# The second layer of two early batches as seven quarter products, on one Trainium2 core

## The chip, the core and the metric

The kernel runs on one core of a Trainium2 chip. Its time is the device time of one execution in microseconds (us); a median of several executions is given, and one execution was recorded by the hardware profiler. The engines of the core are TensorE (PE in the rows, with its weight loads as PEld), VectorE (DVE), ScalarE (ACT), GpSimd (POOL) and SyncE (SP), which here only starts transfers. Each engine works through its own list of instructions in order, and waits where an input or a buffer is not ready. PE writes into eight accumulation banks of 128 rows by 512 float32; ACT and DVE read them and write to the on-chip memory.

## What is computed

For 8 batches of 8 heads with 512 tokens, 32 states and 64 features, tokens read from states and states read from tokens, both by a softmax. The 544 rows of a batch (512 token rows, then 32 state rows) then go through a layer with a maximum of two products, and a last product.

```
scores = scale * x @ state.T          ; scores -= max over states
a = exp(scores) / sum                 ; xread = a @ state
scores2 = scale * state @ x.T         ; scores2 -= max over tokens
a2 = exp(scores2) / sum               ; sread = a2 @ x
X = concat([xread, sread]) as (8 * 544, 512)
out = maximum(X @ w1, X @ w2) @ w_out
```

## The kernel before

**The algebra.** `maximum(X w1, X w2)` is written as `relu(X (w1 - w2)) + X w2`. So the kernel keeps `wd` = w1 - w2, `wwo` = w2 w_out and `wo` = w_out, and the result is `relu(X wd) wo + X wwo`. As xread = a @ state, it multiplies the states into the weights first: `sw` of a batch holds state times `wd` (1,024 columns, the parts 0 and 1 of `sw`) and state times `wwo` (512 columns, the part `w`). Layer one of a batch (`l1_mm`, eight pieces) multiplies `sw` by the transposed attention weights `at`; a relu copies each piece into `r`. Layer two multiplies `r` by `wo` and adds `at` times the part `w` of `sw`.

**Two ways through layer two.** Batches 2 to 7 go through it by a scheme with seven quarter products in place of eight (`product`, `opened`, `keep`, `put`): `r` and `wo` are cut into quarters, sums and differences of quarters are made (`r_sum` into `st`, `w_sum` into `wt`, `difference` into `dif`), three intermediate sums are copied out of the banks (`keep`, into `part`), and four quarters of the output are put together (`put`). Each product is eight matmuls of 256 columns. Batches 0 and 1 go through layer two directly (`l2_mm`): for each of four groups of 128 rows, eight matmuls with `wo` and two with `sw`, all of 512 columns, and one copy out (`l2_out`).

**The order of the work.** The work ahead of the loop over batches 2 to 7 is the list `ORDER`: each token is a call, with the engine behind `>` and the bank numbers behind `@`. `l1.1.5@6` is layer one of batch 1, piece 5, in bank 6; `re.1.5>V` its relu on VectorE; `sw.0.w` the product for the part `w` of batch 0 and `swe.0.w.1>A` the copy of one half of it on ScalarE; `sc`, `exp`, `red`, `mul` are scores, exponential, sums and normalisation; `xtd`, `atd`, `Sd` are transposing transfers, `ldx` loads of `x`, `ce` and `cb` casts of `x`. The list's order is the program order: every engine gets its instructions in it, and an instruction waits for what stands before it in the list and writes what it reads, or reads what it overwrites. `RELEASE` gives the order in which the loop takes up the banks.

**The state rows of batches 0 and 1.** Their numerators and sums are computed early (`srw`) and copied into `srx` (`swre`). They are picked out of it by eight small copies on GpSimd (`srp`, function `sr_pick`) into `srd`, and divided in the loop, with batches 2 and 3 (`sr_ev`). `srx` has no memory of its own: it is a view of the third `sw` buffer, which batch 2 uses as its `sw`.

```
srd = wz.bitcast(F32).rearrange("p (b z) -> p b z", b=2)
srx = sw_s[2].rearrange("p g w -> p (g w)")[:, 0:2080].bitcast(F32).rearrange("p (b g k z) -> p b g k z", b=2, g=2, k=4)
```

`sr_ev` writes the reciprocal of each sum into `rr_all`, which is a part of `sums`. A buffer of batch `b` is number `b % 3` for `sw`, `at` and `xe`, and `b % 2` for `r`, `e`, `a`, `xt` and `xb`.

**The guard and the general block.** The main path leaves out the subtraction of the maximum. So the kernel looks at every sum that it divided by, and at the reciprocals of the state rows:

```
sv = sums[:, 0:B * 34]
nc.vector.tensor_scalar(cl, sv, scalar1=1e-20, scalar2=1e20, op0=ALU.max, op1=ALU.min)
nc.vector.tensor_tensor(ne, cl, sv, op=ALU.not_equal)
nc.vector.tensor_reduce(bad, ne, axis=AXX, op=ALU.max)
```

A matmul adds `bad` over the 128 rows, the integer goes into `flag`, every engine loads it into a register, and behind the last batch stands `with tc.If(fv >= 1, ...)`. The block in it (`general`) does all eight batches again, one after the other, with the maxima subtracted, and the state rows too: each batch is loaded anew through GpSimd's queue into one buffer (`slot["x0"]`), goes through casts, transposes, scores, both softmaxes, `sw`, layer one and the direct layer two, and is stored through GpSimd's queue; the last state rows follow with `m1` and `m2`. In GpSimd's list the two stores of a batch stand ahead of the two loads of the next. In the execution shown below the block was not entered.

**The end.** `m1` and `m2` take the state rows of all batches through both layers in two groups of 128 rows. The last half of the second group is copied by DVE and ACT, 128 columns each.

Of the kernel before, what the change touches and what calls it, by code (L numbers as in the profile page):

```python
# [36 lines left out]
sw.0.0@2,4 re.0.4>V sw.1.0@0,5 swe.0.0.1>A sw.0.w@1,3 swe.1.0.1>V sw.1.w@7,6 ce.2.0>P swe.1.0.0>A l2.1.3.3@4  # L37
swe.1.w.0>V cb.2.1>P l2.1.2.3@5 swe.0.0.0>A l2.1.2.2@5 swe.1.w.1>V swe.0.w.1>A l1.1.2@2 ce.2.3>P xtd.2 mS.1>A
swe.0.w.0>V l2.1.3.2@4 ce.2.1>P l1.0.3@3 l1.0.1@1 re.1.2>A ce.2.2>P l1.1.0@6 re.0.3>A re.0.1>V l2.0.2.2@2 l1.0.6@7
re.1.0>V mS.0>A l1.1.3@1 l1.0.2@6 re.0.6>A Sd l2.0.3.o@3 ldx.4.1 re.0.2>A l2.1.3.o@4 ldx.3.0 l2.0.3.3@3 re.1.3>A  # L40
l1.0.0@6 ldx.4.0 l1.1.1@1 re.0.0>V l2.1.0.o@7 ldx.3.1 l2.1.0.2@7 re.1.1>V l2.0.0.1@6 l2.1.2.0@5 l2.1.0.0@7 l2.1.2.o@5
l2.0.0.o@6 sc.2.0@1 l2.0.3.1@3 exp.2.0>A l2.1.1.3@0 l2.0.2.o@2 red.2.0>V l2.1.3.1@4 l2.1.3.0@4 srp.0>P srp.1>P wt.0>P wt.2>P wt.1>P
mul.2.0>P l2.1.1.1@0 le.1.3>A sc.2.1@1 l2.1.1.2@0 ce.3.0>P exp.2.1>A l2.1.0.1@7 ce.3.1>P l2.0.2.3@2 red.2.1>V
l2.1.2.1@5 cb.3.0>P l2.0.3.0@3 le.1.2>V l2.0.0.3@6 mul.2.1>P l2.1.1.0@0 l2.0.0.2@6 l2.1.1.o@0 ce.3.3>P atd.2
l2.1.0.3@7 ce.3.2>P le.1.1>A l2.0.3.2@3 le.1.0>V l2.0.0.0@6 cb.3.1>P le.0.3>A sr.2@0 le.0.0>V sw.2.0@3,7 xtd.3
ldx.5.0 ldx.5.1
sw.2.w@5,1 sre.2>V swe.2.0.0>A sw.2.1@6,4 l2.0.2.0@2 swe.2.w.1>A swe.2.w.0>V l2.0.1.3@0 swe.2.1.1>A l2.0.2.1@2
swe.2.0.1>V l2.0.1.o@0 le.0.2>A l2.0.1.2@0 swe.2.1.0>A l2.0.1.0@0 srt.2@2 l2.0.1.1@0 srte.2>A le.0.1>V store.0
# [6 lines left out]
RELEASE = [3, 1, 5, 4, 7, 6, 2, 0]  # L55
# [3 lines left out]
def kernel(  # L59
# [9 lines left out]
    nc = tc.nc  # L69
# [494 lines left out]
    for b in range(2):  # L564
        for c in range(NC):
            left[f"l2{b}{c}"] = 5
# [276 lines left out]
```

## Time and profile before

| What | Time |
|---|---|
| median of 3 executions | 147.36 us (147.19 to 147.72) |
| the profiled execution, device time | 147.19 us |
| its span, first to last instruction | 145.4 us |
| PE busy in the span | 136.4 us of 145.4 (94%) |
| DVE, ACT, POOL busy | 98.3, 82.1, 67.9 us |
| last instruction of PE ends, then last of ACT | 140.3 us, 140.9 us |
| `flag` written by DVE | 120.3 us |

The rows of the trace give a start and a duration in us, the engine, the line (`L427` is line 427 of the kernel), the operation, what is written from what is read, and the tiles' sizes. Rows by line give a count, the busy time in us, and the mean of one instruction in ns. The chain of work that ended last is followed back from the last instruction. The 1.8 us between the device time and the span lie around the instructions.

### The profile page before, as it was taken

The numbers are of one execution on the slowest core, as the hardware profiler recorded it, in microseconds if no ns is written. First come the engines' busy times: TensorE is split into PE (matmuls) and PEld (weight loads), VectorE is DVE, ScalarE is ACT, GpSimd is POOL, SyncE is SP. The second block draws the span as 40 slices with busy tenths as digits, with TensorE's granted clock in tenths as the row PEclk, the third lists the DMA queues.
The fourth block names the chain that finished last, engine by engine and source line by source line (L and its number), as shares of the span: only waits on it lengthen the run. The fifth ranks groups of instructions, "written<-read, shape, count | busy, mean of one in ns | idle before, by whom it ended". The sixth has DMA issues, their size and how long they took to land.

```text
span 145.4 us, 3491 instructions
## 1 busy us (share of the span) xinstructions
PE 136.4 (94%) x1376; PEld 89.0 (61%) x1388; DVE 98.3 (68%) x181; ACT 82.1 (56%) x157; POOL 67.9 (47%) x95
## 2 busy tenths in 40 slices
PE   6888999999999999999999999999999999999950
PEld 2566735444454446785778478757867784885840
DVE  3488969783324648997899789489948896941300
ACT  4457789898122675845781768268556817831110
POOL 4147320198979990498079509923930630000000
PEclk9999999999999999999999999999999999999995
DMA  3999999939991599999976991487316034202451
GB/s 126 331 364 394 384 387 385 327 58 174 243 359 59 97 251 393 369 136 275 384 123 138 347 285 33 72 288 149 67 42 252 7 72 185 113 0 72 155 181 38
DMA packets 36468, 29.50 MB, mean 203 GB/s; under 512 B 22624, under 2 KB 32352, under 8 KB 35552
## 3 DMA queue, kind: packets, MB, share of 16 engines
q1 hardware_dynamic: 36176, 29.10, 68.9%
q8 instruction: 12, 0.20, 0.6%
q10 hardware_dynamic: 272, 0.13, 0.3%
q14 instruction: 8, 0.07, 0.2%
HBM read 15.20 MB, written 8.91 MB: 166 GB/s over the span
## 4 chain that ended last, share of the span: by engine, by line
PE 83%; DMA 11%; ACT 1%; issue 1%; DVE 1%; SPq 0%; DVEq 0%
PE bank L427 26%; PE bank L376 19%; PE bank L390 9%; DMA big<-in_moe_w_out_dram 8%; PE bank L433 7%; PE bank L353 4%; DMA big<-in_x_dram 3%; PE bank L578 3%; PE bank L474 2%; PE bank L484 2%; PE bank L385 2%; PE bank L265 2%; PE bank L305 1%; PE bank L482 1%; ACT wo L103 1%
## 5 line engine op out<-in xcount | busy, mean ns | idle before, releaser
L371 DVE TENSOR_SCALAR r<-bank 128x512 bf16<-128x512 f32 x32 | 21.8, 691 | 13.0 <-PE bank L376 12.6
L281 POOL TENSOR_TENSOR a<-e,er 128x512 bf16<-128x512 bf16 x14 | 16.6, 1195 | 29.5 <-ACT e L273 22.5
L376 PE MATMUL bank<-at,sw 128*128 128x512 bf16 x122 | 29.4, 379 | 0.5 <-DVE sw L105 0.2
L103 ACT COPY big<-bank 128x512 f32<-128x512 f32 (+1 forms) x29 | 16.9, 587 | 17.5 <-PE bank L427 6.6
L103 ACT CAST sw<-bank 128x512 bf16<-128x512 f32 x35 | 19.5, 606 | 4.0 <-PE bank L353 4.0
L427 PEld LDWEIGHTS <-big 128*128 128x128 bf16 x192 | 17.9, 98 | 5.1 <-DVE er L278 2.1
L369 ACT ACTIVATE r<-bank 128x512 bf16<-128x512 f32 x32 | 18.5, 597 | 4.5 <-PE bank L376 4.2
L376 PEld LDWEIGHTS <-sw 128*128 128x128 bf16 x128 | 12.3, 98 | 14.1 <-ACT sw L103 0.5
L107 POOL CAST xe<-big 128x512 bf16<-128x512 f32 x27 | 17.7, 688 | 6.2 <-DMA big<-in_x_dram 6.2
L427 PE MATMUL bank<-big,big 128*128 128x256 bf16 x144 | 17.1, 273 | 0.0
L107 POOL CAST xb<-big 128x1024 bf16<-128x1024 f32 x12 | 12.2, 1040 | 7.2 <-DMA big<-in_x_dram 7.2
L390 PE MATMUL bank<-wo,r 128*128 128x512 bf16 x61 | 15.2, 379 | 0.3 <-issue 0.2
L427 PEld LDWEIGHTS <-r 128*128 128x128 bf16 x144 | 13.7, 98 | 2.6
L403 DVE TENSOR_TENSOR big<-bank,big 128x512 f32<-128x512 f32 (+1 forms) x19 | 12.3, 654 | 2.9 <-PE bank L433 2.9
L277 DVE TENSOR_REDUCE sums<-e 128x16 f32<-128x512 bf16 x16 | 10.6, 664 | 5.1 <-ACT e L273 5.0
L103 ACT COPY sread_t<-bank 128x128 bf16<-128x128 bf16 x8 | 3.3, 473 | 16.9 <-PE bank L337 13.7
L273 ACT ACTIVATE e<-bank 128x512 bf16<-128x512 f32 x16 | 9.0, 601 | 5.8 <-PE bank L265 5.7
L427 PE MATMUL bank<-wo,r 128*128 128x256 bf16 x96 | 12.3, 273 | 0.0
L433 PE MATMUL bank<-sw,at 128*128 128x256 bf16 x72 | 10.8, 273 | 0.0
L390 PEld LDWEIGHTS <-r 128*128 128x128 bf16 x64 | 5.9, 98 | 7.0 <-issue 0.5
L433 PEld LDWEIGHTS <-at 128*128 128x128 bf16 x96 | 9.4, 98 | 1.1
L403 DVE TENSOR_TENSOR big<-r 128x1024 bf16<-128x1024 bf16 x12 | 9.2, 767 | 0.6
(86 smaller groups left out, 195.9 us busy)
## 6 DMA issues: line engine op xcount, KB each, us to landing
big<-in_x_dram SPq DMA_DIRECT2D x16, 512.0 KB, 5.5
out_dram<-big SPq DMA_DIRECT2D x7, 1024.0 KB, 5.4
big<-in_moe_w_dram SPq DMA_DIRECT2D x8, 512.0 KB, 11.7
big<-in_moe_w_out_dram SPq DMA_DIRECT2D x4, 512.0 KB, 11.7
out_dram<-big SPq DMA_DIRECT2D x4, 256.0 KB, 3.5
sf<-in_state_dram SPq DMA_DIRECT2D x1, 384.0 KB, 10.4
out_dram<-w2m SPq DMA_DIRECT2D x1, 256.0 KB, 2.5
out_dram<-w2m SPq DMA_DIRECT2D x2, 128.0 KB, 3.1
```

Of the source, the lines that this page charges most:

```text
L103: nc.scalar.copy(o, i)
L107: nc.gpsimd.tensor_copy(o, i)
L273: nc.scalar.activation(out=e_view(e_s[b % 2], hh).rearrange("p (g c) i n -> p g c (i n)", g=2), in_=p.rearrange("p (c g m) -> p g c m", c= ...
L277: nc.vector.tensor_reduce(es_all[:, b, hh], e_view(e_s[b % 2], hh), axis=AXX, op=ALU.add)
L281: (nc.gpsimd if eng == "P" else nc.vector).tensor_mul(e_view(a_s[b % 2], hh), e_view(e_s[b % 2], hh), er_s[b % 2][:, hh].unsqueeze(3).to_b ...
L369: nc.scalar.activation(out=o, in_=p, func=ACTF.Relu)
L371: nc.vector.tensor_scalar(o, p, scalar1=0.0, scalar2=None, op0=ALU.max)
L376: nc.tensor.matmul(p, sw_s[b % 3][:, g, f * 128:(f + 1) * 128], at_s[b % 3][:, g].rearrange("p c t -> p (c t)"), start=(g == 0), stop=(g = ...
L390: nc.tensor.matmul(p[:, lo:hi], r_s[b % 2][:, f, c * 128:(c + 1) * 128], wo[:, f, lo:hi], start=(start and j == 0), stop=(stop and j == le ...
L403: (nc.gpsimd if eng == "P" else nc.vector).tensor_tensor(o, i0, i1, op=op)
L427: nc.tensor.matmul(pv[c], lhs[:, f, 128 * c:128 * c + 128], rhs[:, f, :], start=first and f == 0 and (c == 0 or pv.split), stop=False, ski ...
L433: nc.tensor.matmul(pv[c], at_s[b % 3][:, g, 2 * i + c, :], rhs[:, g, :], start=False, stop=False, skip_group_check=True)
```

## The change

Batches 0 and 1 now go through layer two by seven quarter products as well. New tokens stand for the steps (`p1` to `p7` products, `p2o`, `o7`, `o3`, `o4` the terms with `sw`, `k0` to `k2` the copies into `part`, `rs` and `wt` the sums, `dif` the differences, `v00` to `v10` the outputs), and the second half of `ORDER` is written anew, with other banks and other engines for many copies; `RELEASE` is changed with it. The casts `ce.2` move from POOL to ACT, `wt.2` and `wt.3` from POOL to DVE, and `store.0` stands ahead of `xtd.3`. The state rows are ordered by batch and then by state within `sread_t` and in `m_store`, ACT alone makes the last copy, and the general block's last stores are cut in halves. The pieces of the diff, the list cut to the lines that the text speaks of:

```diff
-swe.0.w.0>V l2.1.3.2@4 ce.2.1>P l1.0.3@3 l1.0.1@1 re.1.2>A ce.2.2>P l1.1.0@6 re.0.3>A re.0.1>V l2.0.2.2@2 l1.0.6@7
-l2.0.0.o@6 sc.2.0@1 l2.0.3.1@3 exp.2.0>A l2.1.1.3@0 l2.0.2.o@2 red.2.0>V l2.1.3.1@4 l2.1.3.0@4 srp.0>P srp.1>P wt.0>P wt.2>P wt.1>P
...
+p1.0@1 k0.0>A p1.1@4 rs.0.2>V wt.2>V v00.0 p6.0 rs.0.3>V k0.1>A k1.0>A p5.0@7 wt.3>V v00.1 rs.1.0>V k2.0>A
+sc.2.0@6 exp.2.0>A sc.2.1@0 exp.2.1>A sw.2.0@5,3 red.2.0>V mul.2.0>P red.2.1>V swe.2.0.0>A swe.2.0.1>A ce.2.0>A ce.2.1>A ce.2.2>A ce.2.3>A
+p7.0 o7.0 v11.0 rs.1.1>V mul.2.1>P p3.0 o3.0 rs.1.2>V atd.2 sw.2.w@6,2 swe.2.w.0>A v01.0 swe.2.w.1>A
+p4.0 o4.0 rs.1.3>V ce.3.0>P ce.3.1>P cb.3.0>P ce.3.2>P ce.3.3>P cb.3.1>P v10.0>A store.0 xtd.3 dif.1>P
+sr.2@0 p6.1 k1.1>A sw.2.1@5,3 sre.2>V swe.2.1.0>A swe.2.1.1>V p5.1@7 k2.1>A srp.0>P srp.1>P
...
-RELEASE = [3, 1, 5, 4, 7, 6, 2, 0]
+RELEASE = [1, 6, 2, 5, 3, 0, 4, 7]
...
-        o = sread_t.rearrange("p k (t n q) -> p k t n q", t=2, q=4)
-        copy(eng, o[:, :, b // 4, :, b % 4], p[:, 0:128].rearrange("p (k n) -> p k n", k=4))
+        o = sread_t.rearrange("p k (t q n) -> p k t q n", t=2, q=4)
+        copy(eng, o[:, :, b // 4, b % 4, :], p[:, 0:128].rearrange("p (k n) -> p k n", k=4))
...
-        (eng or nc.sync).dma_start(out=out.rearrange("(t q l) m -> t l q m", t=2, l=L)[t, S:L, :, lo:hi],
+        (eng or nc.sync).dma_start(out=out.rearrange("(t q l) m -> t q l m", t=2, l=L)[t, :, S:L, lo:hi],
...
+    def fresh(kind, b, lhs, rhs, at):
+        pairs[kind, b] = Pair(at)
+        product(pairs[kind, b], lhs, rhs, True)
...
-    w_sum(3, "P")
...
-    m2(1, "VA", "r", 256, 512)
+    m2(1, "A", "r", 256, 512)
...
-            m_store(t, nc.gpsimd)
+            for k in range(2):
+                m_store(t, nc.gpsimd, 256 * k, 256 * k + 256)
```

POOL's list behind the first casts of batch 2, before. The eight copies `wz0<-sw2` are `srp.0` and `srp.1` (`srd` is a view of `wz`, `srx` one of `sw2`); `big3<-wo0` are the weight sums `wt`, `a0<-e0,er0` is `mul.2`, `xe0` and `xb1` from `big9` are the casts of batch 3, and `big6<-sw2` is `dif` of batch 2:

```order
L107 COPY wz0_73<-sw2_104 32x130 x8
L403 TENSOR_TENSOR big3_112<-wo0_77 128x1024 x2
L403 TENSOR_TENSOR big3_112<-wo0_77,big3_112 128x1024
L281 TENSOR_TENSOR a0_93<-e0_91,er0_95 128x8x64
L107 CAST xe0_84<-big9_118 128x2x4x64 x2
L107 CAST xb1_90<-big9_118 128x4x4x64
L281 TENSOR_TENSOR a0_93<-e0_91,er0_95 128x8x64
L107 CAST xe0_84<-big9_118 128x2x4x64 x2
```

The same stretch of POOL's list now, where a line number is one lower than before:

```order
L402 TENSOR_TENSOR big3_112<-wo0_77 128x1024
L106 CAST xb0_89<-big8_117 128x4x4x64
L402 TENSOR_TENSOR big3_112<-wo0_77,big3_112 128x1024
L402 TENSOR_TENSOR big6_115<-sw0_102 128x512
L280 TENSOR_TENSOR a0_93<-e0_91,er0_95 128x8x64 x2
L106 CAST xe0_84<-big9_118 128x2x4x64 x2
L106 CAST xb1_90<-big9_118 128x4x4x64
L106 CAST xe0_84<-big9_118 128x2x4x64 x2
L106 CAST xb1_90<-big9_118 128x4x4x64
L402 TENSOR_TENSOR big6_115<-sw1_103 128x512
L106 COPY wz0_73<-sw2_104 32x130 x8
L402 TENSOR_TENSOR big6_115<-sw2_104 128x512
```

The eight copies moved from ahead of `mul.2` and the casts of batch 3 to behind them, two weight sums left POOL, and `dif` of batches 0 and 1 (`big6<-sw0`, `big6<-sw1`) came in.

ACT's list around batch 2's scores, before. `e0<-bank` is `exp.2`, `sw2<-bank` are the copies `swe.2` of batch 2's products into the third `sw` buffer, and `big2<-bank`, `big0<-bank` are output copies of batches 1 and 0:

```order
L273 ACTIVATE e0_91<-bank1_64 128x8x64
L103 COPY big2_111<-bank0_63 128x512
L103 COPY big0_109<-bank3_66 128x512
L103 CAST sw2_104<-bank3_66 128x512
L103 CAST sw2_104<-bank1_64 128x512
L103 CAST sw2_104<-bank4_67 128x512
L103 COPY big0_109<-bank2_65 128x512
L103 CAST sw2_104<-bank6_69 128x512
```

ACT's list there now; `big6<-bank` are the copies `k` into `part`, and `xe2` the casts `ce.2`:

```order
L102 COPY big6_115<-bank7_70 128x512
L272 ACTIVATE e0_91<-bank6_69 128x8x64
L272 ACTIVATE e0_91<-bank0_63 128x8x64
L102 CAST sw2_104<-bank5_68 128x512
L102 CAST sw2_104<-bank3_66 128x512
L102 CAST xe2_86<-big8_117 128x2x4x64 x4
L102 CAST sw2_104<-bank6_69 128x512
L102 CAST sw2_104<-bank2_65 128x512
L102 COPY big0_109<-bank1_64 128x2x256
L102 COPY big6_115<-bank4_67 128x512
L102 CAST sw2_104<-bank5_68 128x512
```

Two of the copies into `sw2` now stand directly behind the exponentials, ahead of the casts of batch 2; in the program order of the list all six of them (five on ACT, one on DVE) come before `srp.0`.

More of the change, by code (lines that the diff above doesn't have):

```diff
@@ L46 @@
-ldx.5.0 ldx.5.1
-sw.2.w@5,1 sre.2>V swe.2.0.0>A sw.2.1@6,4 l2.0.2.0@2 swe.2.w.1>A swe.2.w.0>V l2.0.1.3@0 swe.2.1.1>A l2.0.2.1@2
-swe.2.0.1>V l2.0.1.o@0 le.0.2>A l2.0.1.2@0 swe.2.1.0>A l2.0.1.0@0 srt.2@2 l2.0.1.1@0 srte.2>A le.0.1>V store.0
+sw.0.0@2,4 re.0.4>V wt.0>P sw.1.0@0,5 swe.0.0.0>A swe.0.0.1>V sw.0.w@1,3 sw.1.w@7,6 cb.2.1>P swe.1.0.0>A swe.1.0.1>V xtd.2 wt.1>P
+p2.1@2 l1.0.6@4 swe.0.w.0>A re.0.6>V l1.0.3@0 l1.0.2@5 swe.0.w.1>A re.0.3>V swe.1.w.0>V mS.1>A
+l1.0.1@4 l1.0.0@1 p2.0@3 swe.1.w.1>V mS.0>A Sd dif.0>P re.0.2>V re.0.1>A re.0.0>A p2o.0
@@ L563 @@
         left[f"ww{i}"] = 4
-    for b in range(2):
-        for c in range(NC):
-            left[f"l2{b}{c}"] = 5
     def acc(key, ring):
@@ L578, in ww_mm @@
             nc.tensor.matmul(p, w2t[:, f, i, :], wo[:, f, :], start=(first and f % 2 == 0), stop=(last and f % 2 == 1))
[L580 to L585 removed]
+    pairs = {}
+    def fresh(kind, b, lhs, rhs, at):
+        pairs[kind, b] = Pair(at)
+        product(pairs[kind, b], lhs, rhs, True)
     def sw_range(b, z):
```

32 lines of the change are left out of this document (16 added, 16 removed).

## The prediction

> **What bounds the kernel now.** I read the page's first part, then the chain that ended last, then the timelines of PE, POOL and ACT around the rewritten list, then the DMA rows.
>
> ```profile
> PE 136.4 (94%) x1376; PEld 89.0 (61%) x1388; DVE 98.3 (68%) x181; ACT 82.1 (56%) x157; POOL 67.9 (47%) x95
> PE 83%; DMA 11%; ACT 1%; issue 1%; DVE 1%; SPq 0%; DVEq 0%
> 43.88 3.45 PE bank L390 x16
> 70.36 0.87 PE bank L427 x8
> ...
> 79.72 0.44 PE bank L433 x4
> 139.40 0.89 PE bank L484 x8
> 140.63 0.27 ACT w2m L103
> ```
>
> PE is the bound: 83% of the chain. In the chain's rows 16 matmuls of 512 columns take 3.45 us (0.2156 each), and 8 of 256 columns take 0.87 us (0.109 each). So only PE's work and new waits of PE would count, if the main path were all that runs. Here it will not be, and that decides the time.
>
> **The step that decides: the eight copies of the state sums come too late.** `srx`, which holds numerators and sums of the state rows of batches 0 and 1, lies in the first 2,080 of the 3,072 bf16 places in a row of the third `sw` buffer. Four of the six copies `swe.2` overwrite the first 2,048 of them, a fifth the last 32. Before, the copies out stood first:
>
> ```profile
> 32.89 2.62 POOL L107 COPY wz<-sw 32x130 f32<-32x130 f32 x8
> 49.88 1.56 ACT L103 CAST sw<-bank 128x512 bf16<-128x512 f32 x3 [0.63 <-PE bank L353]
> ```
>
> POOL was done with them at 35.5 us, and ACT overwrote the buffer from 49.9 us on. Now the tokens `srp.0` and `srp.1` stand behind all six copies into the buffer, and a reader waits for the last writer ahead of it: the program is free of races, and it reads batch 2's `sw`. Two bf16 numbers of a state times weight product are then taken for a float32 sum. Its sign is that of the upper one, as often negative as positive. `sr_ev` puts the reciprocals of four such words on each of 128 rows into `sums`; a negative one is below 1e-20, so `cl` differs from it, `bad` is 1 on that row, and `flag` is at least 1. That no one of 512 signs is negative can be left out of account. So every engine enters `general` behind the main path, and all eight batches are computed a second time. The span is the main path's plus the block's.
>
> **The main path.** Products: 80 matmuls of 512 columns (17.25 us) become 144 of 256 (15.7 us): 1.6 us less. In the loop the same steps of batch 3, the nine rows of lines 427 and 433 from 70.36 to 79.72 in the chain, take 8.19 us instead of 72 x 0.109 = 7.85, so only 0.9 us may be left; I take 1.2. New waits: DVE gets eight sums, two weight sums and six additions for four copies, some 9 us more, by the row below 16.1 us are busy of 30 now. PE's `p4.0` overwrites a bank that `v11.0` on DVE reads, and two reductions stand ahead of that: laid out by durations of the rows, it waits 0 to 1.1 us.
>
> ```profile
> 24.00:54.00 30.00, 29.67 (x227) 13.71 (x230) 16.09 (x29) 17.37 (x31) 23.85 (x30) 1.00 0.79 202
> L403 DVE TENSOR_TENSOR big<-r 128x1024 bf16<-128x1024 bf16 x12 | 9.2, 767 | 0.6
> 60.17 2.51 POOL L281 TENSOR_TENSOR a<-e,er 128x512 bf16<-128x512 bf16 x2 [5.65 <-DVE er L278]
> 49.23 1.80 SPq L243 DMA_TRANSPOSE xt<-xb  x1
> 57.60 0.63 PE L265 MATMUL bank<-sbd,xt 128*128 128x64 bf16 x16
> L103 ACT COPY big<-bank 128x256 f32<-128x256 f32 x4 | 1.4, 374 | 7.6 <-PE bank L433 5.7 <-PE bank L427 1.9
> 140.31 0.30 DVE w2m L105
> ```
>
> `ce.2` on ACT (4 x 0.62 us) stands ahead of `sr.2` on PE: 0 to 0.3 us. The two weight sums, casts and differences shift POOL by about 2 us, covered by its idle time of 5.65 us ahead of `mul.3`; were that gone, `at` of batch 3 would land late. On SP `store.0` now goes ahead of `xtd.3`, whose `xt` the scores at 57.60 read 8.4 us later, and some 7 now. It lands 4.3 to 10.6 us after its issue (row further below): 0 to 3 us. The last copy by ACT alone costs 0.37 us in place of 0.30 + 0.27: 0.2 us less. The new order of the state rows moves the same bytes in rows of the same length: nothing; a copy of 128x128 costs ACT 0.27 us in the last row of the first fence, beside PE's work, and would cost that if ACT bounded. I take 0.4 us of waits at `p4.0` and `sr.2`, near their low ends, as the rows' durations alone make none: 1.0 us less in all (between 1.8 less and 3.3 more), so the main path ends at 140.9 - 1.0 = 139.9 us.
>
> **The block.** The trace has no execution of it, but nearly every instruction has a near row:
>
> ```profile
> L103 ACT CAST xe<-big 128x512 bf16<-128x512 f32 x3 | 1.9, 618 | 3.5 <-DMA big<-in_x_dram 3.4
> 4.96 0.97 PE L250 MATMUL bank<-ident,xe 128*128 128x128 bf16 x8
> L105 DVE COPY xt<-bank 128x1024 bf16<-128x1024 bf16 x4 | 2.7, 687 | 0.8 <-PE bank L250 0.7
> L640 DVE TENSOR_REDUCE bad<-wb 128x1 bf16<-128x272 f32 x1 | 0.4, 440 | 0.0
> L403 DVE TENSOR_TENSOR big<-bank,big 128x256 f32<-128x256 f32 x2 | 0.8, 420 | 0.5 <-PE bank L433 0.5
> L273 ACT ACTIVATE e<-bank 128x512 bf16<-128x512 f32 x16 | 9.0, 601 | 5.8 <-PE bank L265 5.7
> L277 DVE TENSOR_REDUCE sums<-e 128x16 f32<-128x512 bf16 x16 | 10.6, 664 | 5.1 <-ACT e L273 5.0
> L278 DVE RECIPROCAL er<-sums 128x16 f32<-128x16 f32 x16 | 4.0, 253 | 1.6 <-DVE sums L277 0.5
> L281 DVE TENSOR_TENSOR a<-e,er 128x512 bf16<-128x512 bf16 x2 | 1.5, 728 | 0.1
> 8.02 0.41 PE L265 MATMUL bank<-sbd,xt 128*128 128x64 bf16 x8 [0.34 <-DVE sbd L105]
> 8.46 0.60 ACT L273 ACTIVATE e<-bank 128x512 bf16<-128x512 f32 x1 [1.01 <-PE bank L265]
> 14.91 0.61 PE L292 MATMUL bank<-ident,a 128*128 128x128 bf16 x8
> 48.99 0.43 PE L305 MATMUL bank<-xe,e 128*32 128x65 bf16 x32
> L311 DVE RECIPROCAL sums<-bank 128x2 f32<-128x2 f32 x6 | 0.9, 156 | 0.0
> ```
>
> Its batches can't overlap: GpSimd's list has a batch's stores, which need the last copy of layer two, ahead of the next loads. So a batch costs its whole chain, step by step:
> 1. cast 0.62, eight transposes 0.97, copy 0.69: 2.3 us.
> 2. Twice (DVE runs the halves in order): two maxima 2 x 0.44, two subtractions 2 x 0.42, exponential 0.60, sums 0.66, reciprocal 0.25, product 0.73: 7.9 us.
> 3. Transposes of `a` 0.61, copy 0.69: 1.3 us.
> 4. The second softmax, four times: maximum over 512 (as the sums, 0.66), a scalar 0.16, exponential 0.60, transposes 0.41 (as the scores), the next products 0.4 beside a copy: 2.23, in all 8.9 us.
> 5. State rows 0.43, their division 0.6 (a reciprocal 0.16, two products), a transpose 0.2 (a third of eight), the first `sw` product 0.41 (as the scores), two copies on ACT 1.1: 2.7 us.
> 6. Layer one, 16 matmuls: 3.45 us at full pace, 6.9 at half. I take 5.2.
> 7. Layer two directly, 40 matmuls: 8.6 us. Last copy 0.6.
>
> That is 37.5 us, and about 40 handovers between engines at some 0.05 us (PE's scores end at 8.43, ACT starts at 8.46) make it 39.5; I use 40. Step 6 rests on these rows:
>
> ```profile
> 1.29 3.81 PE L544 MATMUL bank<-wz 128*128 128x256 bf16 x11 [1.29 <-DVE ones L547]
> 7.06 0.62 PE L250 MATMUL bank<-ident,xe 128*128 128x128 bf16 x8 [0.47 <-ACT xe L103]
> ```
>
> The list's first eleven fills have six of 512 and five of 256 columns, 4,352 in all, so 0.88 ns a column; a 512 later takes 0.2156 us, 0.42 ns. And the same eight transposes took 0.97 us at 4.96 and 0.62 at 7.06. PE starts at half its pace and speeds up after some 4 us, though the row of granted clock says 1.00 throughout. In the block PE sits nearly idle through steps 2 to 4 (18 us), so it should be slow again when layer one starts; 5.2 is the middle between both paces. [...]
>
> 8. The turn to the next batch: two stores and two loads issued on GpSimd, and the second load's landing. No row has a DMA issued by GpSimd; the nearest are SP's:
>
> ```profile
> 0.86 2.10 SPq L168 DMA_DIRECT2D big<-in_x_dram  x4
> big<-in_x_dram SPq DMA_DIRECT2D x16, 512.0 KB, 5.5
> out_dram<-big SPq DMA_DIRECT2D x7, 1024.0 KB, 5.4
> DMA to landing us min/median/max: 4.3/6.1/10.6
> ```
>
> Four issues take 2.1 us and a load lands 5.5 us after its own: 7.6, and I take 8 as the loads share the lanes with the stores. The low end is 6 (0.5 + 5.5, the loads not held up by the stores), the high end 12.7 (2.1 and the slowest landing of the trace, 10.6, a transposing transfer behind stores). [...]
>
> For the first batch the load is hidden: POOL can load the flag from 120.4 us on (row below), and nothing else of the main path stands in its list behind that. The second batch's load waits in addition for batch 0's store to land, since both use one buffer: 5.4 us. Behind the eighth batch: `m1` 3.7 + 0.4, `m2` twice 12 matmuls 5.2, copy 0.6, store issue 0.5 and landing 3.1: 13.5 us.
>
> ```profile
> 123.54 3.66 PE L474 MATMUL bank<-sread_t,wd 128*128 128x256 bf16 x32
> 120.30 0.14 DVE L765 CAST flag<-bank 1x1 int32<-1x1 f32 x1
> out_dram<-w2m SPq DMA_DIRECT2D x2, 128.0 KB, 3.1
> ```
>
> Sum: 139.9 + 8 x 40 + 7 x 8 + 5.4 + 13.5 = 534.8, and about 0.5 for the jump (free at the least; at the most a load of instructions, as slow as the fastest transposing transfer, 4.3 us): 535.3 us of span. The profiled execution has 147.19 - 145.4 = 1.8 us around its span, and its 147.19 is 0.17 below the median, so I say **537 us**.
>
> **The rivals.** (a) The guard stays silent: the copies get the old sums after all, because some wait I have not seen holds ACT's copies back, or the words pass the test. Then the main path alone counts: 147.2 - 1.0, about 146 us, faster. The point that decides is whether any word in `rr_all` is negative. For it speaks only that the list was laid out in full; against it the two lists in which both engines' rows stand. (b) The block is cheaper: loads at 6 us (7 x 2 = 14 less), layer one at full pace (8 x 1.75 = 14 less), handovers hidden in the durations (16 less), and maxima and exponentials over 64 rows or half tiles a tenth cheaper (8 x 21 x 0.1 = 17 less): 537 - 61 = 476 us. For it: PE's small bursts in step 4 may keep it at pace. (c) GpSimd's DMAs are dear: four issues at 2.0 us each, as SP's four together, and landings of 10.6: 18.6 a turn, 7 x 10.6 = 74 more, 611 us. For it: no row shows what GpSimd pays to start a transfer of 512 pieces of 1 KB; against it, SP's rows of 0.5. (d) PE stays at half pace through layer two too: 8 x (1.7 + 8.6) = 82 more, 619 us. Against it: over 12 us of unbroken matmuls, three times what the start needed.
>
> **How the numbers follow.** Forecast 0.60, (a) 0.03, (b) 0.14, (c) 0.14, (d) 0.09. The forecast's own range is 505 to 575 us. To hold 8 in 10, I reach to where half of (b) and half of (c) fall in: 485 to 610. What a measurement of this kernel can tell from no change is about 0.3%. Faster has the chance of (a), 0.03; same 0.01, for a main path that gives its gain back while the guard is silent; slower 0.96.
>
> **What would show it.** Right: instructions of lines 647 to 696 in the profile, loads of `x` issued by POOL, a span above 480 us with PE idle over half of it, and eight equal stretches of about 48 us. Step 8 is the gap between the last copy of layer two and the next cast; step 6 the spacing of layer one's matmuls. Main path: PE's last `m2` matmul of lines 481 and 483 ahead of the block near 139 us, with a wait of at most 1.1 us ahead of `p4.0`. Wrong: no instruction of `general`, and a span near 144 us.

## The result, and the profile after

The changed kernel takes 558.94 us (median of 4 runs, 556.62 to 559.76), the kernel before 147.4 us (147.19 to 147.72): 3.789 times as long, with a 95% interval of 3.775 to 3.803. The forecast was 537 us, with a range of 485 to 610. One execution in what follows, of the kernel called rows by place, took 160.9 us at a granted clock of 0.86 and is left out: that kernel then stands at 146.32 us, 1.0 below before, where the expectations written after it say 146.38 and 0.9. The first two parts of the page after, instructions and busy time first, then busy tenths and granted clock in 40 slices of 13.95 us:

```profile
span 558.0 us, 7419 instructions
PE 338.8 (61%) x2960; PEld 199.8 (36%) x2988; DVE 266.5 (48%) x533; ACT 184.7 (33%) x330; POOL 92.2 (17%) x127
PE   7999999999349124922662393349226623922593
PEclk9999999999758655855595577558655955875598
```

PE's row is dense for ten slices, which is the kernel that was written, and then repeats a pattern of low and high digits to the end. That is the block `general`: eight batches, one after the other. PE has 2960 matmuls, where the kernel before had 1376. Its granted clock falls to half in the thin places (0.50 from 256 to 274 us).

ACT's timeline shows where the batches begin and end. On ACT a batch begins with two casts into `xe` and ends with the last copy from a bank into `big`; the first row is the last copy of the main path:

```profile
141.41 0.37 ACT L102 COPY w2m<-bank 128x256 f32<-128x256 f32 x1 [0.94 <-PE bank L483]
141.68 1.14 ACT L102 CAST xe<-big 128x512 bf16<-128x512 f32 x2
...
182.49 0.59 ACT L102 COPY big<-bank 128x512 f32<-128x512 f32 x1 [3.73 <-PE bank L389]
...
194.93 0.62 ACT L102 CAST xe<-big 128x512 bf16<-128x512 f32 x1 [1.35 <-DMA big<-in_x_dram]
...
287.83 0.59 ACT L102 COPY big<-bank 128x512 f32<-128x512 f32 x1 [3.73 <-PE bank L389]
296.67 0.62 ACT L102 CAST xe<-big 128x512 bf16<-128x512 f32 x1 [8.25 <-DMA big<-in_x_dram]
298.10 0.62 ACT L102 CAST xe<-big 128x512 bf16<-128x512 f32 x1 [0.82 <-DMA big<-in_x_dram]
...
540.82 0.59 ACT L102 COPY big<-bank 128x512 f32<-128x512 f32 x1 [3.73 <-PE bank L389]
```

The span is thus made of four kinds of time, each taken from these rows and their like for the other batches. The main path and the first batch's first cast take 142.2. Eight chains, from a batch's second cast to the end of its last copy, take 39.9 to 43.0 us, 330.1 in all. Seven turns, from there to the next batch's second cast, take 11.9 once (182.49 + 0.59 to 194.93) and 9.3 to 9.8 six times (287.83 + 0.59 to 298.10 is 9.7), 69.2 in all. Behind the last batch lie 16.6 us. The sum is 558.1, against 558.0.

### The profile page after: what moved, and what is told of

It is laid out like the page before. It is cut to its first block, busy times and chain, and to the rows that moved or that the text cites. A ratio compares the mean times of both kernels' runs of the same rounds, so it can differ in the third digit from the quotient of the medians.

```text
span 558.0 us, 7419 instructions
## 1 busy us (share of the span) xinstructions
PE 338.8 (61%) x2960; PEld 199.8 (36%) x2988; DVE 266.5 (48%) x533; ACT 184.7 (33%) x330; POOL 92.2 (17%) x127
## 3 DMA queue, kind: packets, MB, share of 16 engines
q1 hardware_dynamic: 36140, 29.10, 18.2%
## 5 line engine op out<-in xcount | busy, mean ns | idle before, releaser
L375 PE MATMUL bank<-at,sw 128*128 128x512 bf16 x240 | 68.2, 430 | 2.9 <-issue 1.8
L249 PE MATMUL bank<-ident,xe 128*128 128x128 bf16 x160 | 18.1, 283 | 73.3 <-ACT xe L102 73.0
L389 PE MATMUL bank<-wo,r 128*128 128x512 bf16 x248 | 60.1, 379 | 0.4
L370 DVE TENSOR_SCALAR r<-bank 128x512 bf16<-128x512 f32 x64 | 44.1, 691 | 29.9 <-PE bank L375 28.8
L368 ACT ACTIVATE r<-bank 128x512 bf16<-128x512 f32 x64 | 37.8, 599 | 23.3 <-PE bank L375 20.4
L249 PEld LDWEIGHTS <-xe 128*128 128x128 bf16 x160 | 13.5, 128 | 79.6 <-ACT xe L102 78.7
L679 ACT ACTIVATE wb<-bank,cm 64x512 bf16<-64x512 f32 x32 | 21.8, 682 | 60.9 <-DVE cm L678 60.9
L375 PEld LDWEIGHTS <-sw 128*128 128x128 bf16 x256 | 27.1, 110 | 39.8 <-issue 20.2
L102 ACT CAST xe<-big 128x512 bf16<-128x512 f32 x23 | 13.9, 625 | 68.5 <-DMA big<-in_x_dram 68.5
L102 ACT CAST sw<-bank 128x512 bf16<-128x512 f32 x60 | 33.4, 600 | 9.1 <-PE bank L352 9.1
L104 DVE COPY big<-bank 128x512 f32<-128x512 f32 (+1 forms) x18 | 11.9, 662 | 41.8 <-PE bank L389 40.7
L104 DVE CAST sw<-bank 128x512 bf16<-128x512 f32 x36 | 23.7, 685 | 10.1 <-PE bank L352 10.1
```

The costliest lines, as they stand in the source:

```text
L102: nc.scalar.copy(o, i)
L104: nc.vector.tensor_copy(o, i)
L249: nc.tensor.transpose(p[:, (c * 2 + kk) * 128:(c * 2 + kk + 1) * 128], xe_s[b % 3][:, c, 2 * hh + kk, 8:136], ident)
L368: nc.scalar.activation(out=o, in_=p, func=ACTF.Relu)
L370: nc.vector.tensor_scalar(o, p, scalar1=0.0, scalar2=None, op0=ALU.max)
L375: nc.tensor.matmul(p, sw_s[b % 3][:, g, f * 128:(f + 1) * 128], at_s[b % 3][:, g].rearrange("p c t -> p (c t)"), start=(g == 0), stop=(g = ...
```

## The experiments

Two questions were open: whether the overwritten buffer alone sends the kernel into the block, and what the main path and the block's parts cost one by one.

### The copies put back ahead of the buffer's new contents

```diff
-l1.0.1@4 l1.0.0@1 p2.0@3 swe.1.w.1>V mS.0>A Sd dif.0>P re.0.2>V re.0.1>A re.0.0>A p2o.0
+l1.0.1@4 l1.0.0@1 p2.0@3 swe.1.w.1>V mS.0>A Sd dif.0>P srp.0>P srp.1>P re.0.2>V re.0.1>A re.0.0>A p2o.0
...
-sr.2@0 p6.1 k1.1>A sw.2.1@5,3 sre.2>V swe.2.1.0>A swe.2.1.1>V p5.1@7 k2.1>A srp.0>P srp.1>P
+sr.2@0 p6.1 k1.1>A sw.2.1@5,3 sre.2>V swe.2.1.0>A swe.2.1.1>V p5.1@7 k2.1>A
```

> The changed kernel with one edit: the two tokens srp.0 and srp.1 stand behind dif.0, ahead of batch 2's scores, so the state sums are copied out before batch 2's products overwrite their buffer. Theory (the late copies alone raise the flag): the block is not entered, POOL makes the copies in the 7.1 us in which it waits for mul.2 (36.5 to 43.6 us in the profile of the changed kernel), and the waits of 0.39, 0.16 and 0.52 us in the loop's first batch go too, since POOL is 2.65 us earlier: 147.4 - 0.7 (the rewritten stretch, 23.5 us instead of 24.3) - 0.2 (last copy) = about 146.5 us, between 145.5 and 147.2. Rival (seven products or the rows by batch raise the flag, by other numbers in the sums): still 555 to 560 us.

Measured: 149.71 us (149.46 to 150.63), 1.0161 times before (1.0131 to 1.019). With two tokens moved, the block is gone, so they are what it hung on. But the main path, which was to be 1 us faster, is 2.4 us slower. The expectation missed, and with it rival (a)'s 146 us. PE's timeline and ACT's of this kernel, then the DMA share and the rate in 40 slices of 0.4 us from 134 to 150 us:

```profile
67.24 3.61 PE L375 MATMUL bank<-at,sw 128*128 128x512 bf16 x15 [1.09 <-DMA at<-a]
...
140.81 0.37 ACT L102 COPY w2m<-bank 128x256 f32<-128x256 f32 x1 [0.94 <-PE bank L483]
```

```profile
DMA  0000013211379999984332222222211100000000
GB/s 0 0 0 0 0 31 31 10 10 38 72 182 287 289 292 335 376 284 156 108 115 97 95 49 49 51 74 74 72 64 49 49 20 0 0 0 0 0 0 0
```

The share in the same view of the kernel before:

```profile
DMA  0000599940980198470154100000000000000000
```

The last copy ends at 141.2, 0.3 us later than before (140.9). But the span ends at 148.8 where it ended at 145.4: the path behind the last copy has grown from 4.5 to 7.6 us. In the slices this is the row of 2s, four microseconds in which a fifth to a quarter of the DMA engines' time is busy and some 50 to 75 GB/s move. Before, the same bytes went in bursts, with digits up to 9. What changed there is the order of the state rows, which the prediction priced at nothing. After the change they stand by batch, the 32 rows of a batch together; before, they stood by place, the rows of one state of four batches together.

### The rows by batch, taken out and put in alone

Out of the kernel of the first experiment:

```diff
-        o = sread_t.rearrange("p k (t q n) -> p k t q n", t=2, q=4)
-        copy(eng, o[:, :, b // 4, b % 4, :], p[:, 0:128].rearrange("p (k n) -> p k n", k=4))
+        o = sread_t.rearrange("p k (t n q) -> p k t n q", t=2, q=4)
+        copy(eng, o[:, :, b // 4, :, b % 4], p[:, 0:128].rearrange("p (k n) -> p k n", k=4))
...
-        (eng or nc.sync).dma_start(out=out.rearrange("(t q l) m -> t q l m", t=2, l=L)[t, :, S:L, lo:hi],
+        (eng or nc.sync).dma_start(out=out.rearrange("(t q l) m -> t l q m", t=2, l=L)[t, S:L, :, lo:hi],
```

> The kernel of the first experiment (late copies moved ahead, guard silent), with the rows of the last state matrices again laid out place by place, so that the last stores' slowest dimension is 32 and not 4. Theory A: the 2.4 us that the first experiment lost lie in the last stores, whose transfer now runs at a quarter of the DMA share (0.20 in the trace where the kernel before has 0.46 to 0.25) and ends 7.6 us behind the last copy instead of 4.5: with the old rows 146.6 to 147.6. Rival B: the rows are harmless and the seven products cost it (their wait of 1.09 us for batch 3's probabilities, and what follows): 149.3 to 150.1, as in the first experiment.

Measured: 146.32 us (median of 11 runs, 145.77 to 147.56), 0.9932 times before (0.9904 to 0.9959). Theory A holds, and the time is a little under its range: the new list with its seven products does make the main path faster, by 1.0 us, and the rows by batch hid it. This kernel beats both.

The same three lines the other way round in the kernel before, with nothing else changed:

> The kernel before with the rows by batch alone, nothing else changed. Theory A: 149.9 to 150.9 (147.4 and some 3 us more behind the last copy). Rival B: 147.1 to 147.7.

Measured: 150.4 us (149.58 to 151.18), 1.0211 times before (1.0173 to 1.0248), 3.1 us more and inside theory A's range. The DMA shares of the two kernels in the same 40 slices, rows by place first:

```profile
DMA  0000000396970893960270180000000000000000
```

```profile
DMA  0000003230259999996334222222111000000000
```

The row of 2s goes with the rows by batch and comes with them. The stores write the same bytes in pieces of the same length. What differs is the order of their dimensions: the slowest one of the output has 32 entries by place, 4 by batch. The first of the three stores can be read alone, before the next transfers start. Its stretch in the first experiment, then in the kernel before (length; busy us and counts of the five engines, granted clock, DMA share, GB/s):

```profile
136.30:138.20 1.90, 1.90 (x19) 1.71 (x18) 0.69 (x1) 0.23 (x1) 0.00 (x0) 1.00 0.25 30
```

```profile
135.80:136.60 0.80, 0.80 (x9) 0.72 (x8) 0.22 (x1) 0.00 (x0) 0.00 (x0) 1.00 0.88 315
```

The share in the first store is 0.25 by batch against 0.88 by place, and the kernel before with rows by batch alone has 0.25 there as well (136.5 to 138.2 us).

The packets in the traces tell few packets in flight apart from slow packets. From 134 to 150 us the first experiment and the kernel before have these:

```profile
DMA packets 1215, 1.34 MB, mean 84 GB/s; under 512 B 60, under 2 KB 1084, under 8 KB 1212
```

```profile
DMA packets 1252, 1.36 MB, mean 85 GB/s; under 512 B 96, under 2 KB 1120, under 8 KB 1248
```

The packets under 512 B are of 4 bytes each. Six stores fall into this stretch: 96 are 16 for each store; 60 are 16 for each of the three stores of token rows and 4 for each of the three by batch. In the trace's list of packets, the 128 of the last store take 46 ns each at the median in all four kernels, by place and by batch. But by place up to 16 or 17 are in flight at once and all pass within 0.6 to 1.4 us; by batch there are hardly ever more than 4, and they need 2.2 to 2.3 us. So the last store's packets are no slower by batch, but fewer of them are in flight. The first store's packets did take longer by batch (130 ns in the mean, against 91), which the number in flight does not explain. On which DMA engines the packets run, the traces do not tell.

### The store by batch, cut into four

```diff
-        (eng or nc.sync).dma_start(out=out.rearrange("(t q l) m -> t q l m", t=2, l=L)[t, :, S:L, lo:hi],
-                                   in_=rs_o[:, t, lo:hi])
+        o = out.rearrange("(t q l) m -> t q l m", t=2, l=L)
+        for q in range(4):
+            (eng or nc.sync).dma_start(out=o[t, q, S:L, lo:hi], in_=rs_o[32 * q:32 * q + 32, t, lo:hi])
```

> The kernel of the first experiment, rows by batch kept, each of the last state stores cut into four, one per batch of 32 rows. Theory A (a slowest dimension of 4 puts the transfer on few DMA engines): each piece has a slowest dimension of 32 again, the transfers run at the full share and are behind only by the three more issues of 0.4 to 0.7 us each: 147.4 to 148.8. Rival B (the scattered rows in memory are slow whatever the shape): 149.5 or more.

Measured: 149.05 us (147.68 to 149.28), between the two expectations. SP's timeline, and the issues of the stretch from 134 us on:

```profile
139.95 4.95 SPq L491 DMA_DIRECT2D out_dram<-w2m  x8
```

```profile
out_dram<-w2m SPq DMA_DIRECT2D x8, 32.0 KB, 1.6
```

Each piece lands 1.6 us after its issue, but eight issues take 4.95 us, where two took 1.85. Most of the eight take 0.3 to 0.6 us, and one takes 1.62, for a reason that the trace does not show. The last copy ends at 141.2 us; SP is then still busy with the four pieces ahead, and starts the last of its own four at 144.5. So what the transfers save goes into issuing. The packets of 4 bytes number 240 from 134 to 150 us here, 16 for each of 15 stores, as many for each piece as for a store by place. That the order of the dimensions costs 3.1 us is shown by taking it out and putting it in. That by batch some 4 packets are in flight, where by place it is up to 16 or 17, is shown by the packets; that theory A's few engines are the reason is not shown, and this time lies between the two theories.

### The last copy by ScalarE alone, in the kernel before

```diff
-    m2(1, "VA", "r", 256, 512)
+    m2(1, "A", "r", 256, 512)
```

> The kernel before with the last copy of the state rows by ScalarE alone, nothing else changed. The kernel of rows by place, which has this and the seven products, is 0.9 us faster than before in the runs, though in the profiled executions the distance from the first state product to the last copy is the same (119.4 against 119.3). Theory A: the copy is worth 0.1 to 0.3 us (0.37 in place of 0.29 + 0.27, which came one after the other) and the products the rest: 147.0 to 147.3. Rival B: the copy is worth the whole, since the last transfer then also comes home sooner (4.5 us from the last copy to the end before, 3.6 with rows by place): 146.2 to 146.6.

Measured: 147.17 us against 147.25, a ratio of 0.9995 (0.997 to 1.0019). The copy is worth nothing that can be told, 0.5 us at the most, and most of the 1.0 us belongs to the new list with its seven products.

### The wait for batch 3's probabilities

The kernel of rows by place still waits where the first experiment did:

```profile
68.00 3.61 PE L375 MATMUL bank<-at,sw 128*128 128x512 bf16 x16 [0.94 <-DMA at<-a]
```

Its `at` stands in SP's list behind the transposition of batch 4's inputs. Exchanged in every pass of the loop:

```diff
-        if b + 2 < B:
-            xt_dma(b + 2)
...
         at_dma(n)
+        if b + 2 < B:
+            xt_dma(b + 2)
```

> The kernel of rows by place, with the loop's transposition of the inputs two batches ahead issued behind the one of the next batch's probabilities instead of ahead of it. Theory A: the 0.73 us that the seven products save are lost in the 1.09 us that TensorE waits for batch 3's probabilities, whose transposition stands behind the other on SP's queue (issued at 62.93, with the probabilities done at 61.94): the wait falls to at most 0.3 and the time is 0.6 to 1.0 us below that of rows by place. Rival B: the queue's own rate and not its order holds the transposition back: the same as rows by place within 0.3 us.

Measured: 146.86 us (146.43 to 147.44), 0.997 times before (0.995 to 0.999): 0.5 us more than rows by place, which neither theory expected (the two intervals overlap a little). The wait is gone, and one like it stands before batch 6's layer one:

```profile
107.83 3.61 PE L375 MATMUL bank<-at,sw 128*128 128x512 bf16 x16 [1.07 <-DMA at<-a]
```

Then exchanged in the first pass alone:

```diff
-        if b + 2 < B:
+        if b + 2 < B and b != 2:
             xt_dma(b + 2)
...
         at_dma(n)
+        if b == 2:
+            xt_dma(b + 2)
```

> The kernel of rows by place with the two transpositions exchanged in the loop's first pass (batch 2) alone. In the kernel that exchanged them in every pass, TensorE's wait of 0.94 us for batch 3's probabilities was gone, and one of 1.07 us for the probabilities of batch 6 had come. Theory A: each exchange acts on its own pass, so the first wait goes and none comes: 0.5 to 0.9 us below rows by place (146.38), 145.4 to 145.9. Rival B: the queue has to give the time back somewhere: a wait of 0.9 to 1.1 us for some later batch's probabilities, and 146.2 to 146.9.

Measured: 146.32 us (145.69 to 146.55), 0.9925 times before (0.9902 to 0.9949).

```profile
21.55 1.45 PE L375 MATMUL bank<-at,sw 128*128 128x512 bf16 x6 [0.17 <-DVE sw L104]
...
79.72 3.61 PE L375 MATMUL bank<-at,sw 128*128 128x512 bf16 x16 [0.18 <-DMA at<-a]
...
139.79 0.37 ACT L102 COPY w2m<-bank 128x256 f32<-128x256 f32 x1 [0.94 <-PE bank L483]
```

In its trace the wait has shrunk to 0.18 us, and from the first layer-one product to the end of the last copy 118.6 us pass (21.55 to 140.16), against 119.4 with rows by place. The trace goes theory A's way; the time does not: it is that of rows by place, 146.32 us, and in rival B's range, though the wait that B asks for did not come. Whether the other executions of rows by place have the wait at all was not seen.

### The late copies in the kernel before

```diff
-l2.0.0.o@6 sc.2.0@1 l2.0.3.1@3 exp.2.0>A l2.1.1.3@0 l2.0.2.o@2 red.2.0>V l2.1.3.1@4 l2.1.3.0@4 srp.0>P srp.1>P wt.0>P wt.2>P wt.1>P
+l2.0.0.o@6 sc.2.0@1 l2.0.3.1@3 exp.2.0>A l2.1.1.3@0 l2.0.2.o@2 red.2.0>V l2.1.3.1@4 l2.1.3.0@4 wt.0>P wt.2>P wt.1>P
...
-swe.2.0.1>V l2.0.1.o@0 le.0.2>A l2.0.1.2@0 swe.2.1.0>A l2.0.1.0@0 srt.2@2 l2.0.1.1@0 srte.2>A le.0.1>V store.0
+swe.2.0.1>V l2.0.1.o@0 le.0.2>A l2.0.1.2@0 swe.2.1.0>A srp.0>P srp.1>P l2.0.1.0@0 srt.2@2 l2.0.1.1@0 srte.2>A le.0.1>V store.0
```

> The kernel before with one edit: srp.0 and srp.1 moved behind the last copy of batch 2's products into the third sw buffer, all else as before; direct second layer for batches 0 and 1. Theory (the late copies alone cost the time): flag raised, main path plus block, 147.4 + about 411 = 558 us, between 553 and 563. Rival (the block is entered for another reason in the changed kernel): 147 to 149 us, the late copies on POOL costing 0 to 1.5 us. In this kernel the main path's state rows of batches 0 and 1 come from the wrong words, and the block computes them again.

Measured: 554.5 us (one run). The two tokens alone, in the old list and with the old products, cost the whole of it; with the first experiment this shows the cause from both sides. The kernel has the rows by place, and so its end also prices them in the block. GpSimd's stores of the state rows here, and then after:

```profile
546.01 0.58 POOL L490 DMA_DIRECT2D out_dram<-w2m  x1 [4.24 <-DVE w2m L105]
548.59 0.56 POOL L490 DMA_DIRECT2D out_dram<-w2m  x1 [1.99 <-DVE w2m L105]
...
out_dram<-w2m POOLq DMA_DIRECT2D x2, 256.0 KB, 2.4
```

```profile
547.91 1.43 POOL L489 DMA_DIRECT2D out_dram<-w2m  x2 [4.24 <-DVE w2m L104]
550.48 1.37 POOL L489 DMA_DIRECT2D out_dram<-w2m  x2 [1.14 <-DVE w2m L104]
...
out_dram<-w2m POOLq DMA_DIRECT2D x4, 128.0 KB, 4.7
```

From the first of these issues to the end of the span it is 6.6 us here (552.6 - 546.01) and 10.1 after (558.0 - 547.91): 3.5 us more for rows by batch in twice as many pieces. In these transfers, too, fewer packets are in flight by batch: by the traces' lists 16 here and 4 to 8 after, where two stores overlap, though a packet takes no longer (0.17 us here, 0.16 after, at the median).

### The block passed over

```diff
-    with tc.If(fv >= 1, preferred_fallthrough_block=True, label="gen"):
+    with tc.If(fv >= 1000, preferred_fallthrough_block=True, label="gen"):
```

> The changed kernel with the block's condition at 1000 in place of 1, which the flag (at most one for each of 128 rows) never reaches: the main path with the late copies, without the block. The state rows of batches 0 and 1 then come from the wrong words. Theory: the block begins where the main path ends, so what is left is the main path of the profile, whose last copy ends at 141.8 us instead of 140.9: 147.4 + 0.9 = 148.3 us, of which 0.5 us is a later transfer of w_out in that one execution, so 147.5 to 148.5. Against e1 this shows what the late copies cost on POOL alone, expected 1.0 to 1.5 us. Rival (the block's transfers and instructions already disturb the main path): as fast as e1, 146.5.

Measured: 150.19 us (149.81 to 151.12), 1.0189 times before (1.0158 to 1.022). This is the changed kernel's main path by itself (the state rows of batches 0 and 1 come from the overwritten words), 2.8 us slower than before. Of these, -1.0 are the new list and +3.1 the rows by batch, as above; the remaining 0.7 us may be the late copies on GpSimd, which the first experiment doesn't have (149.71), though the two intervals overlap. The expectation missed by the same stores, and so did the rival's 146.5.

### The block's transfers issued by SP

```diff
-                load_x(b, g, nc.gpsimd)
+                load_x(b, g, nc.gpsimd if b == 0 else nc.sync)
...
-                store(b, 0, NC if b < B - 1 else last, 256 * k, 256 * k + 256, eng=nc.gpsimd)
+                store(b, 0, NC if b < B - 1 else last, 256 * k, 256 * k + 256, eng=nc.sync)
```

> The changed kernel with the block's loads of batches 1 to 7 and all its stores of token rows started by SP in place of GpSimd. Theory (a turn is four issues of 0.73 to 0.87 us on GpSimd and a landing of 6.7 us): on SP an issue takes 0.53 and a load lands after 5.5 us, so a turn takes about 7.7 us instead of 9.3: seven turns 11 us less, about 548 us (543 to 553). Rival (GpSimd's way of starting transfers costs nothing, and the landing is the memory's own): 556 to 560.

Measured: 549.04 us (one run), inside the expectation. The seven turns come to 63.5 us here, by the same rows of ACT, against 69.2. GpSimd's issues after, then SP's here:

```profile
288.71 1.46 POOL L468 DMA_DIRECT2D out_dram<-big  x2 [47.49 <-ACT big L102]
290.02 1.65 POOL L167 DMA_DIRECT2D big<-in_x_dram  x2
...
big<-in_x_dram POOLq DMA_DIRECT2D x16, 512.0 KB, 6.7
```

```profile
284.03 1.23 SPq L468 DMA_DIRECT2D out_dram<-big  x2
285.31 2.40 SPq L167 DMA_DIRECT2D big<-in_x_dram  x2
...
big<-in_x_dram SPq DMA_DIRECT2D x14, 512.0 KB, 6.4
```

GpSimd issues the four in 3.0 us (288.71 to 291.67), SP in 3.7, and a load lands 6.7 us after its issue, against 6.4. So rival (c) falls. Of the 10 us between the two kernels the turns explain 6, where 11 were expected of them; the others lie in the main path and the chains (326.5 us against 330.1) of two single runs. That the time fell inside the expectation is in part luck.

### The next batch's loads issued ahead

```diff
-                slot[f"x{b}"] = st8
-                load_x(b, g, nc.gpsimd)
+                if b == 0:
+                    slot["x0"] = st8
+                    load_x(0, g, nc.gpsimd)
...
+            if b + 1 < B:
+                slot[f"x{b + 1}"] = big[5] if b % 2 else big[8]
+                for g in range(2):
+                    load_x(b + 1, g, nc.gpsimd)
```

> The changed kernel with the block's loads of the next batch issued right behind the casts of this one, into one of two other buffers, ahead of this batch's stores. Theory (batches stand in a row because GpSimd's list has the stores ahead of the loads): the turn of 9.3 us falls to a handover, about 0.5 us, seven times 8.8 us less, and the wait of the first turn for batch 0's store, 1.5 to 2 us more, goes too: 559 - 63 = 496 us (490 to 503). Nothing else of a batch overlaps, as every engine's list is in order: pitch 42 us a batch. Rival (loads lie beside the batch anyway, or the time of a batch is set by something the turn hides): above 540.

Measured: 487.67 us (one run), 71 less than after. ACT's timeline from the end of the first batch:

```profile
181.80 0.59 ACT L102 COPY big<-bank 128x512 f32<-128x512 f32 x1 [3.73 <-PE bank L389]
182.28 1.14 ACT L102 CAST xe<-big 128x512 bf16<-128x512 f32 x2
...
223.65 1.14 ACT L102 CAST xe<-big 128x512 bf16<-128x512 f32 x2
```

The turn is gone: the next cast starts as the last copy ends, and a batch takes 41.4 us. The seven turns fall from 69.2 us to 2.9 in all, which shows step 8 to be the serial step it was called. The time is 2 us under the expected range: the turns give 66 of the 71 us, and the chains 5 more (325.0 against 330.1), 2 of them in batch 1.

### PE kept busy

```diff
+    def busy(n):
+        p = bank("a")
+        for _ in range(n):
+            nc.tensor.matmul(p, ident, wd[:, 0, 0:512], start=True, stop=True)
...
+            busy(24)
...
+                busy(6)
```

> The changed kernel with matmuls that nothing reads, put into the block where PE waits: 24 of 512 columns behind the scores of a batch, 6 in each of the four rounds of the second softmax. Theory (PE is at half its clock in steps 2 to 5, granted clock 0.50 and 0.69 in the stretches of batch 0, and this costs time in its small matmuls and in layer one): clock near 1.0, layer one 3.5 us instead of 4.5, the transposes and products of the second softmax 0.2 to 0.3 us less each round, some 2 to 2.5 us a batch, 8 batches 16 to 20 us less: about 541 us (537 to 547). [...] Rival (the block is bound by handovers and by DVE and ACT, the clock costs nothing on the path): 556 to 560, or more where the added matmuls delay the transposes.

Measured: 539.16 us (one run), 20 less than after and inside the expectation, with matmuls added that compute nothing. Three stretches of batch 2 after, two from the softmaxes and one in layer two (times; busy us and counts of PE, PEld, DVE, ACT, POOL; the granted clock; DMA share and rate), and one from batch 2's softmaxes here:

```profile
256.00:262.00 6.00, 2.49 (x20) 1.79 (x20) 3.17 (x7) 1.27 (x2) 0.00 (x0) 0.50 0.00 0
262.00:274.00 12.00, 5.60 (x79) 2.70 (x79) 5.33 (x15) 3.46 (x7) 0.00 (x0) 0.50 0.01 2
...
278.00:288.00 10.00, 9.74 (x45) 4.23 (x44) 2.86 (x5) 1.85 (x4) 0.00 (x0) 1.00 0.01 2
```

```profile
252.00:262.00 10.00, 8.20 (x60) 3.90 (x60) 5.33 (x14) 2.63 (x4) 0.00 (x0) 1.00 0.01 2
```

And the groups of the second softmax's products and transposes from 150 us on, after and then here:

```profile
L675 PE MATMUL bank<-xt,sbd 128*64 128x128 bf16 x128 | 20.3, 314 | 0.0
L682 PE MATMUL bank<-ident,wb 64*128 64x64 bf16 x128 | 12.5, 236 | 57.3 <-ACT wb L679 57.3
```

```profile
L681 PE MATMUL bank<-xt,sbd 128*64 128x128 bf16 x128 | 13.3, 227 | 0.0
L689 PE MATMUL bank<-ident,wb 64*128 64x64 bf16 x128 | 9.3, 194 | 12.1 <-ACT wb L686 12.1
```

The granted clock is 0.50 through the second softmax after and 1.00 with PE kept busy, and the same small products fall from 314 to 227 ns. The eight chains fall from 330.1 to 310.7 us, so the half clock in steps 3 to 6 costs at least 2.4 us a batch. Not all of it was removed: in batch 2's layer one the clock still reads 0.73 here (267.5 to 272.2 us), against 0.65 after.

## Why the prediction was right, and where it was not

**The step that decides** held from both sides: moved late in the old list, the two tokens cost 407 us; moved back in the new one, they give 409 back. That it was a negative word which raised the flag, as the prediction argues, no run shows by itself.

**Rows by batch, "nothing"** is the step that failed. It went by bytes and row length, and left out how much of a store is under way at once: by batch hardly ever more than 4 packets, by place up to 16 or 17. The order of dimensions costs 3.1 us in the main path (1.0211 alone) and some 3.5 with its extra issues in the block's tail, which took 16.6 us where 13.5 were said. Without the guard the forecast for the main path, 1.0 us less, would have come out as 2.4 to 2.8 more, on the other side of no change; and rival (a) would have been 150, not 146.

**The products** came out in size: 1.2 less, 0.4 of waits and 0.2 less for the last copy make 1.0 less, and rows by place measured 1.0 less. But the terms are not shown one by one, and the agreement is in part luck. The last copy alone measured 0.1 with an interval across nothing. From the first layer-one product to the end of the last copy rows by place take 119.4 us, before 119.3, in the profiled executions; with the wait for `at` nearly gone it is 118.6. The waits came elsewhere than said: none ahead of `p4.0`, and 0.5 to 1.1 us for batch 3's `at`, which the prediction named as what would be late were POOL's idle time gone, though it stood behind SP's queue. In the changed kernel's profiled execution the main path ended at 141.8, not 139.9; a later start of 0.5 us (the first state product at 29.61, before at 29.10) is in that, as are the waits. The 0.5 us for the jump rested on no row, and no run shows it: ACT's first cast of the block starts at 141.68 us, where the main path's last copy ends at 141.78.

**The block, step by step**, on batch 2 from PE's timeline:

```profile
247.91 1.04 PE L249 MATMUL bank<-ident,xe 128*128 128x128 bf16 x8 [0.40 <-ACT xe L102]
...
257.75 1.03 PE L291 MATMUL bank<-ident,a 128*128 128x128 bf16 x8 [7.35 <-DVE a L280]
258.72 0.64 PE L675 MATMUL bank<-xt,sbd 128*64 128x128 bf16 x4
261.43 0.63 PE L675 MATMUL bank<-xt,sbd 128*64 128x128 bf16 x4
...
273.77 0.61 PE L375 MATMUL bank<-at,sw 128*128 128x512 bf16 x1
...
279.00 0.59 PE L384 MATMUL bank<-sw,at 128*128 128x512 bf16 x2
```

- Step 4: a round of the second softmax repeats after 2.7 to 2.8 us (258.72 to 261.43 the first), where 2.23 were said; four make 2 us more. The products there ran at half clock, and their row came from full pace; with PE kept busy a round repeats after 2.4 us, so the clock is some two thirds of the miss. The exponential took 682 ns where 0.60 us was said, and the handovers the rest.
- Step 5 took 4.1 us (269.71 to 273.77), 1.4 more than said. With PE kept busy it took 3.6, so a third of the miss is the clock.
- Step 6: 273.77 to 279.00 is 5.2, as said; in batch 1 it was 4.5 (224.04 to 228.55), and over the eight batches 4.0 to 5.5, 5.0 in the mean. The matmuls come 0.43 us apart up to 277.2 us and 0.22 apart from 277.5 on: they do start at half pace, as the prediction had it.
- Step 7: layer two took 8.6 us, at granted clock 1.00, as said. Rival (d) falls.
- The chains came to 330.1 us instead of 320: 41.3 a batch. The misses of steps 4 and 5 are larger than that, and the 2.5 us that the prediction added for handovers took up the rest. The clock is one term that was too small: the prediction allowed 1.75 us a batch for it, all in layer one, and PE kept busy saved 2.4, in batch 2 two thirds of it in steps 4 and 5. The trace has the small matmuls of steps 3 to 5 at half clock too (0.50 in 256 to 274 us).
- Step 8: 9.3 to 9.8 us where 8 was said; the first turn, with its wait for the store, took 11.9 where 13.4 were. Together that is 69.2 us where 61.4 were said. Two loads behind two stores end 6.7 us after their issue, not 5.5; that this comes from lanes shared with the stores, for which the prediction went from 7.6 to 8, no run shows by itself.

The four misses make the difference between the spans: 142.2 instead of 140.4 to the first cast, 10.1 in the chains, 7.8 in the turns, 3.1 in the tail, 22.8 in all, of 558.0 - 535.3 = 22.7. Rival (b) fell: the turns were longer, not shorter; layer one took 5.0 us in the mean, not 3.45; and of the rows a few were a little cheaper (the maxima 415 ns against 440), while the exponentials were dearer.

## What to carry to other kernels

Where instructions are moved in a list, ask of every buffer that is a view of another what is written to it between the old place and the new: a program without races can still read the wrong contents, and here the guard turned that into 3.8 times the time. When a store's rows are laid out anew, compare the slowest dimension of the output, not only bytes and row length (here 4 in place of 32 cost 3.1 us), and look at the DMA share in the last microseconds (0.25 against 0.88 in the first of these stores). A saving off to the side of a guard or a store is only visible when that part is undone by itself: here 1.0 us of gain lay under 3.1 us of loss and 409 us of recomputation.

## What was not expected of the hardware

- A store of 128 rows with a slowest dimension of 4 held the DMA share at 0.25, with 4 packets in flight, where one of 32 had 0.88 and some 16. The packets of the last store took 46 ns in both, and the kernel ended 3 us later.
- Cutting it gave back only 0.7 of the 3.1 us: issues on SP took 0.41 us at the median for 32 or 64 KB and 0.55 for 128 or 256 KB, so that four small ones are dearer than a large one.
- The granted clock read 0.50 from 256 to 274 us of the changed kernel, where PE is busy for 8.1 of 18.0 us, and the second softmax's small products took 1.4 times as long as with PE kept busy (314 against 227 ns); 48 matmuls that compute nothing shortened a batch by 2.4 us.
- In batch 1 alone, DVE stood still for 2.43 us ahead of a product of the first softmax, with nothing in the trace that released it. With PE kept busy the same 2.43 us stand at the same place. In both a transfer of 8 KB of instructions starts within the pause (at 205.54 us after, where DVE stands from 204.85 to 207.28); whether it is the cause stays open.
